# Issuing more feed-forward matmuls as 32-column tiles in a fused attention and feed-forward kernel: from pair 8 on instead of 14

## The chip, the cores and the metric

The kernel runs on one core of one Trainium2 chip. The metric is device microseconds (us) of one execution. Each execution also has a span: the time from its first to its last instruction. It is mostly about 1.8 us shorter than the execution's time. In this document "PE" is TensorE, "DVE" VectorE, "ACT" ScalarE, "POOL" GpSimd and "SP" SyncE. A verdict calls two kernels the same when they are within 2%, so nearly all that follows happens inside "same". It is told because the pieces are not small: a gain and a loss of about 1 us each meet in one place.

## The reference, cut to what matters

```python
q, k, v: (8, 12, 448, 64) float32            # batch, heads, sequence, head dim
scores = q @ k.T / 8;  attn = softmax(scores);  x = attn @ v
x = x.transpose(0, 2, 1, 3).reshape(3584, 768)
g = x @ w_gate;  val = x @ w_val             # (768, 1536) each
out = (g * sigmoid(g) * val) @ w_out         # (1536, 768)
```

There are 96 heads, worked through as 48 pairs. The 3584 rows of x go through the feed-forward part in eight blocks of 384 or 512 rows.

## The kernel before

TensorE's order is written by hand. For each pair `pr` it runs half of the scores (`s`), then in even pairs the row sums of an earlier pair and in odd pairs value products of an earlier pair (`acc`), then some feed-forward steps, then the other half of the scores, and so on. The scores use 64 rows of the array and 128 columns. The sums and value products are issued as four column tiles of 128 rows by 32 columns:

```python
def pv(p0, t, pool=None):
    ...
    for c in range(NC):
        for j in range(4):
            nc.tensor.matmul(acc[ts(j, 32), 0:S], lhsT=v16[g][...], rhs=E[...][:, c, j % 2, :],
                             start=(c == 0), stop=(c == NC - 1))
```

A feed-forward matmul is either one 128x128 matmul or the same work cut into four 128x32 tiles:

```python
def mm(dst, lhsT, rhs, start, stop):
    if not tiled[0]:
        nc.tensor.matmul(dst, lhsT=lhsT, rhs=rhs, start=start, stop=stop)      # line 261
        return
    for j in range(4):
        nc.tensor.matmul(dst[ts(j, 32), :], lhsT=lhsT[:, ts(j, 32)], rhs=rhs,  # line 264
                         start=start, stop=stop)
```

The switch is set in the loop over pairs:

```python
work = odd and pr > FIRST + 1                 # value products in both halves of the pair
...
tiled[0] = pr >= TILED                        # first run, behind sums or value products
carry = ffn_run(...)
...
tiled[0] = pr >= TILED and work               # second run, only in odd pairs
carry = ffn_run(...)
```

The softmax here doesn't subtract the row's maximum and nothing guards it: scores larger than these inputs give would overflow.

## Time and profile before

| what | value | where from |
|---|---|---|
| time, three runs | 463.16 us (462.67 to 463.72) | timed runs |
| span of the profiled execution | 460.2 us | page |
| PE busy | 452.3 us, 98% | page, part 1 |
| next engine | ACT, 53% | page, part 1 |
| chain that ended last | PE 95% | page, part 4 |
| DMA share in the stage changed (pairs 8 to 13) | 1.38 | windows |

PE holds the chain. A busy PE does not mean that PE can't get faster: its records overlap and their ends are modelled. What counts is the distance between the starts of two blocks in the timeline. The DMA share of 1.38 says that in this stage all 16 DMA engines are busy, with more than one packet at a time in the records.

### The profile page before, as it was taken

What the parts mean: (1) busy time and instruction counts of PE and PEld (TensorE: products, weight loads), DVE (VectorE), ACT (ScalarE), POOL (GpSimd) and SP (SyncE); (2) the same over time, 40 slices, a digit from 0 to 9 for tenths busy, and PEclk for the clock granted to TensorE, in tenths of its full rate; (3) what the DMA queues carried; (4) which work ended last, traced back from release to release, by engine and by line L of the source; (5) the groups of instructions that cost most, each with busy time, mean ns of one, the idle gap of its engine ahead of it and who ended that gap; (6) DMA issues with size and microseconds to landing.
All of it is one profiled execution on the core that took longest, in us unless ns stands there. A gap on an engine that the chain in (4) does not pass through costs nothing.

```text
span 460.2 us, 14133 instructions
## 1 busy us (share of the span) xinstructions
PE 452.3 (98%) x6367; PEld 227.8 (49%) x6367; DVE 236.8 (51%) x371; ACT 243.0 (53%) x353; POOL 104.2 (23%) x164
## 2 busy tenths in 40 slices
PE   8899999999999999999999999999999999999996
PEld 3344444444455555444455555544445556554454
DVE  2765663666764554564654554636555546334310
ACT  7986666656664555454646555455555562222222
POOL 8455606334150132303123040210200000000000
PEclk9999999999999999999999999999999999999999
DMA  9999999995793484662758393903603111100123
GB/s 133 195 200 201 192 180 183 223 154 80 90 113 57 78 126 49 114 102 31 118 58 119 67 131 74 142 6 76 98 10 56 37 37 36 36 11 25 36 68 103
DMA packets 82045, 44.23 MB, mean 96 GB/s; under 512 B 36673, under 2 KB 78529, under 8 KB 81985
## 3 DMA queue, kind: packets, MB, share of 16 engines
q0 software_dynamic: 42368, 23.37, 39.2%
q1 hardware_dynamic: 39520, 19.92, 23.8%
q8 instruction: 49, 0.80, 0.7%
q14 instruction: 12, 0.09, 0.1%
q10 hardware_dynamic: 96, 0.05, 0.0%
HBM read 47.19 MB, written 11.01 MB: 126 GB/s over the span
## 4 chain that ended last, share of the span: by engine, by line
PE 95%; ACT 3%; DMA 1%; DVE 0%; issue 0%; SPq 0%; ACTq 0%
PE gp L264 15%; PE op L261 14%; PE vp L264 13%; PE vp L261 11%; PE op L264 10%; PE s L196 10%; PE gp L261 9%; PE acc L212 9%; PE acc L234 4%; ACT E L203 2%; DMA rk<-in_k_dram 1%; PE tp L184 1%; PE wp L103 0%; PE tp L167 0%; DVE qkT L175 0%
## 5 line engine op out<-in xcount | busy, mean ns | idle before, releaser
L203 ACT ACTIVATE E<-s 112x896 f16<-112x896 f32 x192 | 164.6, 917 | 24.3 <-PE s L196 24.1
L280 ACT ACTIVATE sg<-gp 128x384 f32<-128x384 f32 (+1 forms) x96 | 52.3, 545 | 85.4 <-PE gp L264 54.7
L292 DVE SCALAR_TENSOR_TENSOR t<-sg,gp 128x384 f32<-128x384 f32 (+1 forms) x96 | 58.5, 610 | 64.3 <-ACT sg L280 64.2
L325 ACT ACTIVATE osb<-op 128x384 f32<-128x384 f32 (+1 forms) x57 | 27.7, 486 | 100.5 <-PE op L261 56.3
L264 PE MATMUL gp<-X,wg 128*32 128x512 f16 (+1 forms) x1416 | 78.1, 355 | 0.0
L249 DVE RECIPROCAL R<-ssb 128x112 f32<-128x112 f32 x92 | 73.1, 827 | 0.7
L295 DVE SCALAR_TENSOR_TENSOR hts<-t,vp 128x384 f16<-128x384 f32 (+1 forms) x96 | 59.6, 621 | 23.3 <-PE vp L264 7.9
L261 PE MATMUL op<-wo,hts 128*128 128x384 f16 (+1 forms) x408 | 68.6, 322 | 0.0
L264 PE MATMUL vp<-X,wv 128*32 128x512 f16 (+1 forms) x1224 | 66.9, 353 | 0.0
L226 DVE TENSOR_TENSOR X<-acc,R 128x448 f16<-128x448 f32 x48 | 29.7, 624 | 64.9 <-PE acc L212 63.1
L261 PE MATMUL vp<-X,wv 128*128 128x384 f16 (+1 forms) x270 | 58.4, 352 | 0.0
L196 PE MATMUL s<-qkT 64*128 64x448 f16 x384 | 54.8, 355 | 2.5 <-ACT E L203 2.2
L261 PEld LDWEIGHTS <-hts 128*128 128x128 f16 x408 | 38.9, 98 | 28.2 <-issue 3.0
L264 PEld LDWEIGHTS <-wg 128*32 128x32 f16 x1416 | 37.8, 97 | 29.6
L264 PE MATMUL op<-wo,hts 128*32 128x384 f16 x1104 | 48.9, 326 | 0.0
L261 PE MATMUL gp<-X,wg 128*128 128x384 f16 (+1 forms) x222 | 47.4, 350 | 0.0
L264 PEld LDWEIGHTS <-wv 128*32 128x32 f16 x1224 | 32.7, 97 | 25.5
L212 PE MATMUL acc<-E,vt 112*32 112x448 f16 x768 | 45.2, 355 | 0.0
L126 POOL DMA_DIRECT2D vt<-in_v_dram x16 | 12.3, 772 | 142.7 <-PE acc L212 141.7
L261 PEld LDWEIGHTS <-wv 128*128 128x128 f16 x270 | 25.3, 98 | 26.9 <-issue 4.8
L264 PEld LDWEIGHTS <-hts 128*32 128x32 f16 x1104 | 29.5, 97 | 16.3
L154 POOL COPY qk<-q 112x512 f16<-112x512 f16 x37 | 22.9, 620 | 63.9 <-DMA qkT<-qk 46.4
(38 smaller groups left out, 201.2 us busy)
## 6 DMA issues: line engine op xcount, KB each, us to landing
vt<-in_v_dram POOLq DMA_DIRECT2D x16, 336.0 KB, 5.2
q<-in_q_dram POOLq DMA_DIRECT2D x22, 224.0 KB, 5.9
k<-in_k_dram POOLq DMA_DIRECT2D x22, 224.0 KB, 6.7
out_dram<-osb SPq DMA_DIRECT2D x7, 336.0 KB, 3.1
wg<-in_moe_w_gate_dram POOLq DMA_DIRECT2D x8, 288.0 KB, 11.1
wv<-in_moe_w_val_dram POOLq DMA_DIRECT2D x8, 288.0 KB, 11.4
wo<-in_moe_w_out_dram POOLq DMA_DIRECT2D x2, 1152.0 KB, 21.6
out_dram<-osb SPq DMA_DIRECT2D x8, 288.0 KB, 2.9
```

Of the source, the lines that this page charges most:

```text
L154: nc.gpsimd.tensor_copy(dst, src)
L196: nc.tensor.matmul(s[:, hx, 0:S], lhsT=t[ts(hx, 64)].rearrange("p c q -> p (c q)")[:, c * P : c * P + 128], rhs=t[ts(hx, 64), NC:, :].rear ...
L203: nc.scalar.activation(E[pr][:, c], s[0:P, :, 0:S], AF.Exp, scale=sm_scale)
L212: nc.tensor.matmul(acc[ts(j, 32), 0:S], lhsT=v16[g][:, 2 * r + j % 2, c, :].rearrange("p (d t) -> p t d", t=2)[:, t], rhs=E[p0 + j // 2][: ...
L226: nc.vector.tensor_tensor(X[kk][:, hp + t, ts(bb, S)], acc[:, 0:S], R[p0][:], ALU.mult)
L249: lambda i=i: nc.vector.reciprocal(rt[:, ts(i, P)], ssb[:, ts(i, P)]) for i in range(4)
L261: nc.tensor.matmul(dst, lhsT=lhsT, rhs=rhs, start=start, stop=stop)
L264: nc.tensor.matmul(dst[ts(j, 32), :], lhsT=lhsT[:, ts(j, 32)], rhs=rhs, start=start, stop=stop)
L280: nc.scalar.activation(sg[:, 0:n], gp[:, 0:n], AF.Tanh, scale=0.5)
L292: nc.vector.scalar_tensor_tensor(t1[:, 0:n], sg[:, 0:n], 1.0, gp[:, 0:n], ALU.add, ALU.mult)
L295: nc.vector.scalar_tensor_tensor(hts[:, fb, 0:n], t1[:, 0:n], 0.5 * HS, vp[:, 0:n], ALU.mult, ALU.mult)
L325: nc.scalar.activation(osb[:, ds(m0, w)], op[:, 0:w], AF.Copy, scale=1.0 / HS)
```

## The change

A block that follows the 32-column sums or value products in the same tiling should not have to drain the array first. A step from one cutting of the array to another (128x128, 128x32, 64x128) between two matmuls that follow each other is called a mode change below. So the switch to tiles is made six pairs earlier:

```diff
-TILED = 14
+TILED = 8
```

## The prediction

> **What bounds the kernel now.** I read the page first: part 1 (busy time of each engine) and part 4 (the chain that ended last).
>
> ```profile
> PE 452.3 (98%) x6367; PEld 227.8 (49%) x6367; DVE 236.8 (51%) x371; ACT 243.0 (53%) x353; POOL 104.2 (23%) x164
> ...
> PE 95%; ACT 3%; DMA 1%; DVE 0%; issue 0%; SPq 0%; ACTq 0%
> ```
>
> TensorE (PE) is busy for 98% of the 460.2 us span and makes 95% of the chain; the next engine is at 53%. The page warns that ends of matmuls are modelled, so "busy" alone does not say that nothing can be gained inside it. So I took next the waits of PE over the whole run, then the windows view over the stage that the change touches (pairs 8 to 13, which run from 42.27 us, the row sums of pair 8, to 82.58 us, the first scores of pair 14):
>
> ```profile
> PE s L196 <- ACT E L203: 2.2, 5, 0.4
> PE acc L234 <- ACT E L203: 0.4, 1, 0.4
> ...
> 42.27:82.58 40.31, 40.31 (x362) 19.00 (x360) 22.65 (x37) 25.41 (x36) 17.95 (x27) 1.00 1.38 184
> ```
>
> The first two lines are waits in total, their number, and the longest. All of them are before 27 us in the timeline; the waits view restricted to 36 to 90 us lists none. The last line gives busy PE, weight load, DVE, ACT and POOL in us, then the granted clock, DMA share and GB/s. PE is busy in all 40.31 us, at full clock; VectorE has 17.7 us and ScalarE 14.9 us to spare. So what one TensorE block costs is the distance between the starts of two blocks, and that is what I took from the timeline of PE. First the present form in the stage touched:
>
> ```profile
> 56.53 0.94 PE L234 MATMUL acc<-E,ones 112*32 112x448 f16 x16
> 57.41 1.15 PE L261 MATMUL vp<-X,wv 128*128 128x384 f16 x6
> 58.39 1.14 PE L261 MATMUL gp<-X,wg 128*128 128x384 f16 x6
> 59.46 0.55 PE L196 MATMUL s<-qkT 64*128 64x448 f16 x4
> ...
> 62.49 0.94 PE L212 MATMUL acc<-E,vt 112*32 112x448 f16 x16
> 63.36 1.15 PE L261 MATMUL vp<-X,wv 128*128 128x384 f16 x6
> 64.35 2.11 PE L261 MATMUL op<-wo,hts 128*128 128x384 f16 x12
> 66.39 0.55 PE L196 MATMUL s<-qkT 64*128 64x448 f16 x4
> ```
>
> Then the same two patterns later, where the kernel already issues the feed-forward blocks as 32-column tiles (L264, four times as many matmuls):
>
> ```profile
> 158.53 0.94 PE L212 MATMUL acc<-E,vt 112*32 112x448 f16 x16
> 159.30 2.13 PE L264 MATMUL op<-wo,hts 128*32 128x384 f16 x48
> 161.25 1.15 PE L264 MATMUL vp<-X,wv 128*32 128x384 f16 x24
> 162.33 0.55 PE L196 MATMUL s<-qkT 64*128 64x448 f16 x4
> ...
> 360.71 0.94 PE L212 MATMUL acc<-E,vt 112*32 112x448 f16 x16
> 361.48 1.15 PE L264 MATMUL gp<-X,wg 128*32 128x384 f16 x24
> 362.46 1.15 PE L264 MATMUL vp<-X,wv 128*32 128x384 f16 x24
> 363.54 0.55 PE L196 MATMUL s<-qkT 64*128 64x448 f16 x4
> ```
>
> The first column is the start in us. Value products or sums, two 384-wide steps, then scores: 59.46 - 56.53 = 2.93 us untiled and 363.54 - 360.71 = 2.83 us tiled. Value products, one 384-wide step and one output chunk: 66.39 - 62.49 = 3.90 untiled and 162.33 - 158.53 = 3.80 tiled. Tiling takes 0.10 us off a segment, whichever it is. The reader should see where: the 16 matmuls of the acc block are followed after 0.87 to 0.88 us by an untiled block and after 0.77 us by a tiled one. The steps are equally long in both forms (57.41 to 58.39 and 361.48 to 362.46, both 0.98), and so is the exit to the scores (58.39 to 59.46: 1.07; 362.46 to 363.54: 1.08).
>
> **What the Trainium skill says.** (1) "TensorEngine Tiling (Array Packing)", Key Properties: changing the tiling mode, not merely the tile, drains the TensorE. The trace agrees: 0.10 us more where 128x32 is followed by 128x128, and none where 128x32 follows itself. (2) Same page, Restrictions: column tiling disables Fast Weight Load. If that showed, tiled steps would be longer; the trace has one weight load at 97 ns tiled and 98 ns untiled (rows of PEld), and no longer step, so it is hidden here. (3) "TensorE: Matmul & The Clock Gate", Back-to-back issue gap: N / 2.4 + 2.5 ns warm, which is 162.5 ns for 384 columns; the trace has 0.98 us / 6 = 163 ns untiled and the same step as 24 tiled matmuls, 40.8 ns each. (4) Same page, Part 1: a start-to-start floor of about 25 ns, and some 62 ns of ucode per matmul when hardware decode is off. At 40.8 ns the trace is above the first and below the second, so neither floor binds at this width.
>
> **The change, part by part.** The diff lowers one constant, so the first feed-forward run of each pair 8 to 13, and the second one of the odd pairs, is issued tiled; these are the runs that directly follow a sums or value-product block. The second run of the even pairs follows scores and stays untiled.
>
> - *Added instructions.* The instruction order of the built kernels shows 13420 rows on PE in place of 12736. That is 684 more, 342 matmuls and 342 weight loads: 114 untiled matmuls become 456. Their cost is 0, by the equal step lengths above.
> - *Moved.* Nothing. ACT's order is the same; the differences on DVE, POOL and SP are only buffer numbers.
> - *Removed.* The nine blocks in the timeline of before that hold these 114 matmuls start at 43.14, 50.58, 54.00, 57.41, 63.36, 67.75, 71.16, 77.11 and 80.53 us: eight of 12 matmuls and one of 18. Each follows an acc block, and each loses one drain. Counting mode changes along the PE order gives 217 before and 208 after, so nine fewer, none added.
> - *Sum.* The nine distances from acc to untiled add up to 7.86 us (six of 0.87, three of 0.88: 5.22 + 2.64 = 7.86). Eight such distances in the already tiled stretch from 141 to 178 us average 0.767 us; 9 x 0.767 = 6.90. The gain is 7.86 - 6.90 = 0.96 us, 0.107 each.
>
> All of this lies on the path: PE waits for nothing between 27 us and the end, so what it saves early moves all that follows forward. Predicted span 460.2 - 0.96 = 459.2 us; predicted time 463.16 - 0.96 = 462.2 us, that is 0.2%.
>
> **Rivals.**
>
> *A data wait takes the gain back.* This stage has the DMA saturated (share 1.38 above, digits of 9 throughout), so TensorE could run into transfers that do not come sooner. I took each landing (start of the issue plus time to landing) against its first use. Output weights, first half: issued at 44.77, landing 18.1 us later, at 62.9; first used at 64.35. PE will be there five drains sooner, 0.53 us, so 1.5 us of slack becomes 0.95. Second half: 45.8 + 25.0 = 70.8, used at 73.70: 2.9 us. Transposed q and k of pair 11: 48.01 + 9.9 = 57.9, used at 62.01, 4.1 us; pair 14: 73.65 + 4.4 = 78.05, used at 82.58, 4.5 us; pairs 12, 13 and 15 have 6 us or more. All exceed the largest shift, 0.96 us. If the output weights landed 2 us later, about 1 us would be lost and the time would stay at 463.2. I give this 5%.
>
> *Instruction fetch becomes the bound.* Four times as many instructions per us, in the stage with the busiest DMA. Against it: the stage from 82 to 116 us has tiled blocks already and a nearly saturated DMA, and its pitch is that of an unhindered stage:
>
> ```profile
> 94.91 1.47 PE L264 MATMUL gp<-X,wg 128*32 128x512 f16 x24
> 96.21 1.47 PE L264 MATMUL vp<-X,wv 128*32 128x512 f16 x24
> 97.61 0.55 PE L196 MATMUL s<-qkT 64*128 64x448 f16 x4
> ```
>
> The distances 1.30 and 1.40 recur at 340 us with the DMA nearly idle (338.58, 339.88, 341.17, 342.57). The page of that window counts 4 packets of the instruction queue in 34 us; 684 added rows at 256 to a 16 KB packet (64 bytes each, an estimate from 49 packets, 0.80 MB and 14133 instructions) are fewer than 3 packets more. If a fetch did stall PE by about 1 us each, the gain would go and the time would be 463 to 465. I give this 4%.
>
> *Another engine becomes the bound.* The stage gets 0.96 us shorter, 2.4% of 40.31; ACT, the next busiest at 25.41 us, has 14.9 us of idle. PSUM buffers are released in the same order as before, and the tiled stage from pair 14 on, with the same buffers, has no PE wait. It would make the time 462.2 to 463.2; 2%.
>
> *A larger gain.* Were tiled steps themselves shorter by, say, 5%, the 114 matmuls at 163 ns (18.6 us) would yield 0.9 us more, 461.3. The equal steps speak against it.
>
> **Range and chances.** The arithmetic gain is sharp, the times less so: the three runs of before spread from 462.67 to 463.72, so a median of a few runs may be off by 0.4 us on either side, in before and after alike. I put 0.7 us on each side: 461.5 to 462.9. Two per cent is 9.3 us, ten times the gain, and no rival comes near it on either side: faster 0.01, same 0.98, slower 0.01.
>
> **What would show it right or wrong.** Right: acc to L264 distances of 0.76 to 0.77 us at the nine places; tiled 384-wide steps of 0.98 us and chunks of 1.96; 208 mode changes; the scores of pair 14 at 81.6 us in place of 82.58; no PE wait between 30 and 100 us; every later block 0.96 us earlier; a span near 459.2. Wrong: a PE or PEld wait ended by the output weights near 63.8 us, a gap within a tiled block beside an instruction packet, tiled 384-wide steps longer than 0.98 us in this stage, or a shift that is there at 82 us and gone before the end.

## More of the kernel before

Weights are loaded on the way, in an order given by pair. `wo` are the two halves of `w_out`, 1152 KB each as written in float16, and "V" is a group of values (336 KB):

```python
wq = {..., 4: [("g", 3), ("v", 3), ("qk", 12)],
      6: [("V", 3), ("o", 0)],
      7: [("o", 1)]}
```

The first matmul that reads `wo` is an output product of the first block of rows, in the first feed-forward run of pair 11. "The first use of wo" below means this one.

## The result

| | before | changed |
|---|---|---|
| median, six runs each | 463.37 us | 462.40 us |
| range | 462.67 to 463.72 | 462.14 to 463.02 |
| ratio | | 0.9982 (95%: 0.9970 to 0.9995) |
| span of the profiled execution | 460.2 us | 460.4 us |

Ratios throughout are the mean time of one kernel's runs over that of the other's of the same rounds, so not quite the ratio of the medians quoted.

The gain of the medians is 463.37 - 462.40 = 0.97 us; 0.96 was predicted. But the profiled execution of the changed kernel is not shorter than that of before: 460.4 against 460.2 us. Both facts need an explanation, and the agreement of 0.97 with 0.96 turned out to be the less meaningful of the two.

First the page of the changed kernel, parts 1 and 4:

```profile
PE 451.4 (98%) x6709; PEld 229.4 (50%) x6709; DVE 236.8 (51%) x371; ACT 243.0 (53%) x353; POOL 104.2 (23%) x164
...
PE 85%; DMA 12%; POOL 2%; issue 1%; ACT 0%; POOLq 0%
```

There are 342 matmuls more, as foreseen. The chain is new: before it was PE 95% and DMA 1%; now DMA is 12% of it. Something on PE waits for a transfer. The timeline of PE shows the drains first (start in us, duration, engine, line, shapes):

```profile
56.20 0.94 PE L234 MATMUL acc<-E,ones 112*32 112x448 f16 x16
56.97 1.15 PE L264 MATMUL vp<-X,wv 128*32 128x384 f16 x24
57.95 1.15 PE L264 MATMUL gp<-X,wg 128*32 128x384 f16 x24
59.03 0.55 PE L196 MATMUL s<-qkT 64*128 64x448 f16 x4
```

From the sums to the tiled block it is now 0.77 us in place of 0.88, and the whole segment takes 59.03 - 56.20 = 2.83 us in place of 2.93, with steps of 0.98 us as before. The drain is gone as predicted. A few microseconds on, still in the timeline of the changed kernel:

```profile
62.05 0.94 PE L212 MATMUL acc<-E,vt 112*32 112x448 f16 x16
62.82 1.15 PE L264 MATMUL vp<-X,wv 128*32 128x384 f16 x24
64.88 2.13 PE L264 MATMUL op<-wo,hts 128*32 128x384 f16 x48 [0.91 <-DMA wo<-in_moe_w_out_dram]
66.95 0.55 PE L196 MATMUL s<-qkT 64*128 64x448 f16 x4
```

The output product should start 0.98 us after the value step, at 63.80. It starts at 64.88, 1.08 us late, because wo has not landed (0.91 us is the part without any earlier matmul still in the records). The windows view over the same pairs, from the sums of pair 8 to the first scores of pair 14, agrees:

```profile
42.25:82.72 40.47, 39.56 (x704) 20.72 (x704) 22.65 (x37) 25.42 (x36) 17.98 (x27) 1.00 1.41 177
```

The stage takes 40.47 us against 40.31: nine drains fewer, minus 0.96, and one wait more, plus 1.08, make plus 0.12, and 40.31 + 0.12 = 40.43; the rest is rounding and the spread of single distances.

Why does wo land late? The view of wo's transfer, restricted to its first half, gives the start of the issue and the time to landing, first in before, then in the changed kernel:

```profile
L142 POOL DMA_DIRECT2D wo<-in_moe_w_out_dram x1: 1037/1037/1037, 44.8 to 44.8; - x1
DMA to landing us min/median/max: 18.1/18.1/18.1
```

```profile
L142 POOL DMA_DIRECT2D wo<-in_moe_w_out_dram x1: 1037/1037/1037, 44.2 to 44.2; - x1
DMA to landing us min/median/max: 20.6/20.6/20.6
```

It is the same transfer. It was issued 0.5 us sooner and landed 2.0 us later, at 64.8 in place of 62.8 us. The DMA view from 52 to 60 us, in 40 slices of 0.2 us (busy share of the DMA engines in tenths, then GB/s), shows one place where much more time is lost than in before (a shallower dip near 54 us is in both). Before:

```profile
DMA  9999999997999999999999999999999999999999
GB/s 193 189 223 218 179 187 172 173 151 47 173 210 178 184 211 178 184 207 182 182 210 182 180 206 188 195 192 191 188 192 192 189 188 196 186 192 196 188 191 192
```

Changed:

```profile
DMA  9999999999569999999994019999999999999999
GB/s 216 177 192 219 179 170 182 189 132 74 28 87 187 197 187 261 183 177 173 168 36 17 6 14 175 200 184 205 192 192 197 186 191 193 188 192 192 189 188 196
...
q8 instruction: 1, 0.02, 0.7%
```

In the changed kernel there is a hole of four slices near 56 us: 36, 17, 6 and 14 GB/s in place of some 190, with the DMA engines idle (digits 4, 0, 1). About 0.7 us of transfer is lost there. The last line is a packet of the instruction queue, q8, which this window of before does not have. The trace has it at 55.0 us, 1 us ahead of the hole. TensorE now issues more instructions in the same time, and the next packet of them comes sooner. Both kernels have another such hole between 62.7 and 64.4 us, behind the next instruction packet. In before wo has landed by the time most of it comes; in the changed kernel wo is still under way. With slices of 0.55 us over 44 to 66 us, the changed kernel's 136, 27 and 103 GB/s there are some 0.9 us short of 190. So these two holes make about 1.6 of the 2.0 us (an estimate from the slices).

### The profile page after: what moved, and what is told of

It reads as the page before. It is cut to its first block, busy times and chain, and to the rows that moved or that the text cites. A ratio compares the mean times of both kernels' runs of the same rounds, so it can differ in the third digit from the quotient of the medians.

```text
span 460.4 us, 14817 instructions
## 1 busy us (share of the span) xinstructions
PE 451.4 (98%) x6709; PEld 229.4 (50%) x6709; DVE 236.8 (51%) x371; ACT 243.0 (53%) x353; POOL 104.2 (23%) x164
## 4 chain that ended last, share of the span: by engine, by line
PE 85%; DMA 12%; POOL 2%; issue 1%; ACT 0%; POOLq 0%
PE gp L264 15%; PE vp L264 13%; PE op L261 12%; PE op L264 12%; PE vp L261 9%; PE s L196 8%; PE acc L212 7%; PE gp L261 7%; DMA wv<-in_moe_w_val_dram 5%; DMA wo<-in_moe_w_out_dram 4%; PE acc L234 4%; DMA wg<-in_moe_w_gate_dram 2%; POOL q L117 1%; POOL k L117 1%; POOL vt L126 0%
## 5 line engine op out<-in xcount | busy, mean ns | idle before, releaser
L264 PE MATMUL gp<-X,wg 128*32 128x512 f16 (+1 forms) x1512 | 82.7, 353 | 0.0
L264 PE MATMUL vp<-X,wv 128*32 128x384 f16 (+1 forms) x1344 | 72.7, 351 | 0.0
L264 PE MATMUL op<-wo,hts 128*32 128x384 f16 x1344 | 59.5, 326 | 0.9 <-DMA wo<-in_moe_w_out_dram 0.9
L261 PE MATMUL op<-wo,hts 128*128 128x384 f16 (+1 forms) x348 | 57.9, 321 | 0.0
L196 PE MATMUL s<-qkT 64*128 64x448 f16 x384 | 54.8, 355 | 2.5 <-ACT E L203 2.2
L261 PE MATMUL vp<-X,wv 128*128 128x512 f16 (+1 forms) x240 | 52.7, 356 | 0.0
L264 PEld LDWEIGHTS <-wv 128*32 128x32 f16 x1344 | 35.9, 97 | 27.4
L264 PEld LDWEIGHTS <-hts 128*32 128x32 f16 x1344 | 35.8, 97 | 21.1 <-DMA wo<-in_moe_w_out_dram 1.3
L261 PEld LDWEIGHTS <-hts 128*128 128x128 f16 x348 | 33.4, 98 | 23.3 <-issue 1.5
L261 PE MATMUL gp<-X,wg 128*128 128x384 f16 (+1 forms) x198 | 42.8, 352 | 0.0
L246 DVE COPY ssb<-acc 128x448 f32<-128x448 f32 x23 | 14.4, 625 | 40.9 <-PE acc L234 40.9
```

Source lines behind the costliest of these rows:

```text
L196: nc.tensor.matmul(s[:, hx, 0:S], lhsT=t[ts(hx, 64)].rearrange("p c q -> p (c q)")[:, c * P : c * P + 128], rhs=t[ts(hx, 64), NC:, :].rear ...
```

## The experiments

Twelve kernels ran, in three calls of four. Each call had its own runs of before on the same chip, shared by its four kernels. As the effects are a few tenths of a us, I read the spans of all executions as well as the medians: a span does not contain the start of the program.

### Is the gain repeatable, and is wo the cause of the scatter?

`b_again` and `a_again` are the two kernels unchanged. `b_early` and `a_early` load the first half of wo one place sooner:

```diff
-            6: [("V", 3), ("o", 0)],
+            6: [("o", 0), ("V", 3)],
```

Expected of `b_again`:

> The kernel before, unchanged, as a null and for a second profile with the span of each run. Theory A (drains only; nothing waits for the output weights in the usual run of before): spans near 460.2 us as in the first profile, no PE wait after 27 us. Theory B (the first half of the output weights, wo, is a gate: it lands near 64.8 us in most runs and the first profile was a lucky one): spans of 461.2 to 461.9 us, and unless the profile is lucky again a PE wait on wo of about 1 us near 64 us. Time ratio 1.000.

Of `a_again`:

> The changed kernel, unchanged, again. Theory A: nine drains of 0.107 us saved in full, 0.96 us below the null. Theory B: TensorE waits for wo in both kernels, so the five drains saved ahead of the first output matmul are absorbed by the wait and only the four behind it count: 4 x 0.107 = 0.43 us below the null; a PE wait on wo about 0.5 us longer than that of the null.

Of `b_early`:

> The kernel before with the load of wo's first half issued ahead of one load of values (336 KB) instead of behind it. Theory B: wo lands some 2 us or more earlier, no PE wait on it, span near 460.2 us, 1.0 to 1.6 us below the null. Theory A: the same time as the null within 0.3 us.

Of `a_early`:

> The changed kernel with the same earlier load. Both theories: no wait on wo and all nine drains saved, so 0.96 us below b_early (span near 459.2 us). Theory B also: 1.2 to 1.8 us below a_again. Theory A: the same as a_again within 0.3 us.

| kernel | median us | ratio to before (95%) | spans of the six runs |
|---|---|---|---|
| before, 11 runs | 463.05 | | 460.4 to 461.8 |
| b_again | 462.32 | 0.9988 (0.9975 to 1.0000) | 460.2 to 460.6 |
| a_again | 462.56 | 0.9993 (0.9980 to 1.0005) | 460.6 to 461.0 |
| b_early | 463.87 | 1.0017 (1.0003 to 1.0031) | 460.8 to 462.5 |
| a_early | 465.98 | 1.0057 (1.0036 to 1.0078) | 461.8 to 465.3 |

The null, an unchanged copy, taught most. It differs from before by at least as much as `a_again` does, although its text is that of before. The changed kernel's spans lie close together, those of before spread by 1.4 us. The profile of `a_again` has the wait on wo again (1.0 us, at 65.14 us); that of `b_again` has none.

Both early kernels are slower, where theory B expected a gain. The waits view says why (us in total, times, longest), `b_early` first:

```profile
PE acc L212 <- DMA vt<-in_v_dram: 1.5, 1, 1.5
```

```profile
PE acc L212 <- DMA vt<-in_v_dram: 3.0, 1, 3.0
```

The values that were pushed back are needed at 62.67 us, by the value products of pair 8, whose accumulator holds pair 9 as well. In `b_early` they landed at 44.4 + 20.1 = 64.5. I had moved one transfer past another that was nearly as urgent. And the 3.0 us wait in `a_early` cost more than itself. In the windows view (the number behind the engines is the granted clock) the two microseconds after it ran at half clock:

```profile
66.00:68.00 2.00, 2.00 (x28) 1.10 (x24) 0.87 (x2) 0.00 (x0) 0.00 (x0) 0.50 1.28 192
```

So these two say nothing on what a kernel without the wait would do; the next group does.

### The wait taken away, and the drain measured alone

In these four the first block's output product reads gate weights that landed long ago in place of wo. Shapes, instructions and transfers stay the same. The 384 rows of that block come out wrong.

```diff
-    rhs=wo[oh][:, fb, ds(m0 - oh * OH, w)],
+    rhs=(wgv["g", oh][:, fb % NCB] if first else wo[oh][:, fb])[:, ds(m0 - oh * OH, w)],
```

`b_nogate` is before with this edit and `a_nogate` the changed kernel. `untiled_nogate` has, besides,

```diff
-TILED = 8
+TILED = 99
```

and `all_nogate` tiles the second run of the even pairs too, which stands between two score blocks and so keeps its two mode changes:

```diff
-            tiled[0] = pr >= TILED and work
+            tiled[0] = pr >= TILED
```

Expected of `b_nogate`:

> The kernel before, with the output product of the first block of rows reading gate weights that landed long ago in place of wo (same shapes, same instructions, same transfers; 384 of the 3584 rows come out wrong on purpose). Theory B (the landing of wo is what makes the time of before scatter by 1.5 us and what swallows part of the gain): no wait on wo, and all spans within about 0.3 us of 460.3. Theory A (the scatter has another source): spans scatter from 460.3 to 461.8 as before.

Of `a_nogate`:

> The changed kernel with the same replacement (wrong on purpose in the same rows). Theory B: the whole gain of nine drains appears, 0.96 us below b_nogate: spans near 459.3 us, with the scores of pair 14 about 0.96 us earlier than in b_nogate. If a drain is worth less than 0.107 us or tiled steps are longer in this stage, the difference is smaller though nothing waits.

Of `untiled_nogate`:

> a_nogate with no feed-forward step tiled at all (constant 99 in place of 8): 271 mode changes on TensorE in place of 208. If a drain of 0.107 us for each mode change is the whole cost: 63 x 0.107 = 6.7 us more than a_nogate (span near 466.0). If the gain came from something else about the tiles it need not scale with the count.

Of `all_nogate`:

> a_nogate with the second run of the even pairs tiled as well: 1134 matmuls and as many weight loads more, but only two mode changes fewer (206). If only mode changes count: 0.2 us below a_nogate at most. If tiling itself made a step shorter, or the instructions cost something (fetch, issue), it would be off by more: 1134 extra matmuls at even 5 ns each would be 5.7 us.

| kernel | mode changes on PE | median us | ratio to before (95%) | spans, sorted |
|---|---|---|---|---|
| before, 11 runs | 217 | 462.34 | | 460.3 to 461.7 |
| b_nogate | 217 | 463.37 | 1.0010 (0.9996 to 1.0025) | 460.3, 460.6, 461.5, 461.6, 461.7, 461.9 |
| a_nogate | 208 | 461.89 | 0.9987 (0.9974 to 1.0001) | 459.4, 459.5, 459.6, 460.6, 460.8, 460.9 |
| untiled_nogate (4 runs) | 271 | 468.11 | 1.0125 (1.0111 to 1.0138) | 466.1, 466.1, 466.5, 467.2 |
| all_nogate | 206 | 462.52 | 1.0002 (0.9984 to 1.0020) | 459.5, 459.9, 460.7, 460.8, 461.9, 462.2 |

Three things follow.

The scatter is not made by wo. `b_nogate` has no wait on it and still has two groups, near 460.4 and 461.7. Its profile fell on a slow execution (span 461.9), and by 14 us it is 1.63 us behind the first profile, which is nearly all of the 1.7 us between their spans. The same three instruction groups in the timeline, before (quick) and then `b_nogate` (slow):

```profile
5.08 0.39 PE L103 MATMUL wp<-warm 128*128 128x512 f16 x1
5.64 0.75 PE L196 MATMUL s<-qkT 64*128 64x448 f16 x4 [0.16 <-DVE qkT L175]
6.32 0.39 PE L103 MATMUL wp<-warm 128*128 128x512 f16 x1
```

```profile
5.53 0.61 PE L103 MATMUL wp<-warm 128*128 128x512 f16 x1
6.08 0.95 PE L196 MATMUL s<-qkT 64*128 64x448 f16 x4
6.96 0.61 PE L103 MATMUL wp<-warm 128*128 128x512 f16 x1
```

A warm-up matmul takes 0.39 us in one and 0.61 in the other, until about 10 us. The page "TensorE: Matmul & The Clock Gate" of the Trainium skill, Part 1, says that the window which releases the clock runs freely, so that the warm-up ends at another point in each run. These traces agree with it: their records of the granted clock begin, at full clock, at 4.4 us in before and at 10.5 us in `b_nogate`, and there the durations change. (The windows view gives 1.00 before that too, but nothing is recorded there.) In the 14 profiles the record begins at 4.1 to 5.7 us in ten and at 9.4 to 10.5 us in four, those of `b_nogate`, `all_nogate`, `a_split` and `halved`. I call the two kinds quick and slow starts. A quick start is worth some 1.2 us in the means below and 1.6 in these two profiles. Nothing in the change touches it.

Compared within a kind, the whole gain appears once nothing waits: 460.45 - 459.50 = 0.95 us in quick starts (means of two and three spans) and 461.68 - 460.77 = 0.91 in slow ones (four and three). Predicted: 0.96. Against all executions of before, the median of `a_nogate` is only 0.45 us lower, because the two drew different shares of quick starts.

And the drain has its size. Sixty-three mode changes more cost 466.1 - 459.5 = 6.6 us in quick starts, and 63 x 0.107 = 6.7. What the 0.107 us consist of was not separated. In the trace of before, the first weight load behind the sums starts with its block, at 57.40 us, and takes 95 ns; in the changed kernel the first loads start 0.19 us ahead of theirs. So a weight load that cannot go ahead may be a large part of it. In `all_nogate`, 1134 more matmuls at nearly the same count of changes leave the quickest span where it was (459.5 against 459.4), but its median is 0.6 us above that of `a_nogate`, so the added instructions are not free in every execution. The profiled execution of `all_nogate` is a slow one, 462.2, with two gaps on PE of 0.7 and 0.5 us inside the stage; one of them, within a block at 71.09 us, has no releaser but "issue". They may be waits for instructions; that was not settled.

### Where the loss comes from, and a version without it

`post_only` tiles in addition only the four blocks behind the first use of wo, `pre_only` only the five ahead of it:

```diff
 # post_only                                    # first run, then second run of a pair
-            tiled[0] = pr >= TILED
+            tiled[0] = pr >= 12
-            tiled[0] = pr >= TILED and work
+            tiled[0] = pr >= 11 and work
 # pre_only
-            tiled[0] = pr >= TILED
+            tiled[0] = 8 <= pr <= 11 or pr >= 14
-            tiled[0] = pr >= TILED and work
+            tiled[0] = (8 <= pr <= 10 or pr >= 14) and work
```

`a_split` is the changed kernel with the first half of wo in two tiles, loaded one after the other:

```diff
+    wo0b = consts.tile([128, 4, OH], FP16, name="wo0b")   # wo[0] keeps 8 of 12 row groups
...
+            if i == 0:
+                nc.gpsimd.dma_start(dst[:], src[:, 0:8])
+                src, dst = src[:, 8:12], wo0b
...
-    rhs=wo[oh][:, fb, ...]
+    rhs=(wo0b[:, fb - 8] if oh == 0 and fb >= 8 else wo[oh][:, fb])[...]
```

`halved` is before with twice the instructions and no tiles in the first block's gate and value steps:

```diff
-            for cb in range(NCB):
+            for x0, cb in [(x0, cb) for x0 in range(0, n, n // parts) for cb in range(NCB)]:
                 mm(
-                    gp[:, 0:n],
+                    gp[:, ds(x0, n // parts)],          # parts = 2; the same for vp
```

Expected of `post_only`:

> Only the four blocks behind the first use of wo are tiled as well (second run of pair 11, pairs 12 and 13); 213 mode changes. Theory C (by now: a drain is worth 0.107 us wherever it goes; the instructions that tiling adds ahead of the first use of wo bring one more instruction packet into the flight of wo and delay its landing by about 2 us; the scatter of about 1.4 us between executions is made in the first 10 us): no added packet, so wo lands 18 to 19.5 us after its issue as in before, no PE wait on it, and four drains are saved in full: 0.43 us below the kernel before in executions with the same start, spans near 460.0 us with a quick start and 461.3 with a slow one. That is better than the whole change with a quick start (460.6). Theory D (tiles are worth more or less than their drains, instructions do not matter): between before and the changed kernel.

Of `pre_only`:

> Only the five blocks ahead of the first use of wo are tiled as well (pairs 8 to 10 and the first run of pair 11); 212 mode changes. Theory C: wo lands about 20.7 us after its issue, near 65 us, PE waits about 1 us for it with a quick start, and the five drains are lost: spans 460.9 to 461.2 us, 0.5 to 0.8 us ABOVE the kernel before with a quick start, in spite of five drains fewer. Theory D: 0.53 us below before.

Of `a_split`:

> The changed kernel with the first half of wo in two pieces, two thirds and one third, loaded one after the other; the last third is needed 1.3 us later than the first. Theory C: the two thirds land some 2 us before the whole (near 63) and the wait is gone or below 0.3 us: spans 459.4 to 459.8 us with a quick start, 460.8 with a slow one, about 0.9 us below the kernel before. Theory D: no change against the changed kernel (460.6).

Of `halved`:

> The kernel before with the 144 matmuls of the first block's gate and value steps issued as two halves of 192 columns each: 144 matmuls and weight loads more ahead of the first use of wo, no tiles, the same 217 mode changes. Theory C: a third instruction packet between 44 and 66 us, about 0.15 to 0.2 MB less data moved in that window, and wo lands 20 to 21 us after its issue in place of 18.1 to 19.3. Rival E (the delay of wo comes from the tiles themselves, which read their moving operand four times, and not from instructions): wo lands 18 to 19.5 us after its issue as in before. TensorE itself may be up to 1 us slower here, as there are more and shorter matmuls.

| kernel | median us | ratio to before (95%) | spans, sorted | wo: issue + flight = landing | PE wait on wo |
|---|---|---|---|---|---|
| before, 11 runs | 463.33 | | 460.3, 460.3, 460.5, 460.6, then seven from 461.5 to 461.8 | | |
| post_only | 462.03 | 0.9979 (0.9963 to 0.9995) | 459.7, 459.8, 459.9, 460.5, 460.6, 460.8 | 44.9 + 18.2 = 63.1 | none |
| pre_only | 462.82 | 0.9996 (0.9981 to 1.0010) | 460.9 to 461.2, all six | 44.9 + 20.1 = 65.0 | 0.9 us |
| a_split | 461.36 | 0.9967 (0.9948 to 0.9985) | 459.1, 459.4, 459.5, 459.7, 460.8, 460.9 | first piece 43.8 + 17.1 = 60.9 | none |
| halved | 463.19 | 1.0009 (0.9992 to 1.0025) | 461.2 to 462.4 | 44.9 + 19.6 = 64.5 | none |

`post_only` and `pre_only` tell the two theories apart. Four drains fewer behind the first use of wo bring spans of 459.7 to 459.9 in quick starts, where before has 460.3 to 460.6. Its other three, 460.5 to 460.8, are 0.5 us or more below the 461.3 that I expected of slow starts; no profile fell on one of them, so this miss stays open. Five drains fewer ahead of it bring 460.9 to 461.2: more drains saved, and worse than before in quick starts. The timeline of `pre_only` at the place:

```profile
65.08 2.13 PE L264 MATMUL op<-wo,hts 128*32 128x384 f16 x48 [0.86 <-DVE hts L295]
```

The view names DVE here, which is the other thing this matmul needs. But the vp step before it starts at 63.06, so it would start at 64.04 without a wait; it starts at 65.08, just behind the landing of wo at 65.0. This is a wait for several semaphores put down to the wrong one.

`halved` has no added tiles, and still a hole. Its DMA view from 52 to 60 us:

```profile
DMA  9999999999999972089999129999999999999999
GB/s 195 192 211 189 191 187 220 253 177 168 161 83 182 123 23 12 10 131 166 178 204 108 17 15 147 184 189 200 184 189 200 183 195 193 202 184 184 207 182 184
```

Idle slices at 54.8 to 55.4 us follow an instruction packet at 53.5; those at 56.4 to 56.8 us follow a packet of 8 KB of another instruction queue, q14, at 54.6. Two of my expectations for it failed: there were two instruction packets from 44 to 66 us, not three, and wo flew 19.6 us, not 20 to 21. So it shows that such a hole comes without added tiles. By itself it does not show that instructions make the whole delay: 19.6 us is longer than any flight in an untiled kernel (18.1 to 19.3), but shorter than those of the tiled ones (20.1 to 20.9). The rival, that the tiles themselves slow the transfers, is not needed for the hole.

Put together, the times of the wo flight in all profiles where it was loaded whole and in its place are: untiled up to its landing (before, b_again, b_nogate, untiled_nogate, post_only) 18.1, 19.3, 18.6, 18.4, 18.2 us; tiled ahead of it (changed, a_again, a_nogate, all_nogate, pre_only) 20.6, 20.7, 20.9, 20.8, 20.1. The two groups do not overlap. In each of the first five the trace has two packets of the instruction queue from 44 to 66 us, in each of the second five three. The early kernels, where wo is not in its place, look different: it flew 18.5 us in `b_early` and 18.4 in `a_early`, which has one packet more in the flight. But `a_early` issued it 1.1 us later, and it landed 1.0 us later (61.4 against 60.4).

The DMA packets of the traces tell more. For each flight, the time that the DMA fell short of 190 GB/s can be added up (in slices of 0.1 us). It is 0.3 to 1.0 us in the first five, 1.4 in `halved` and 1.7 to 2.7 in the second five. The flight less this time is 17.8 to 18.3, 18.3 and 18.1 to 19.0 us. So of the 2.1 us between the means of the two groups, 1.6 are time in which the DMA stood idle or nearly so; for the other 0.5 the rival stays open.

Not every instruction packet leaves a hole. The DMA view of the changed kernel from 68 to 74 us has a packet, at 69.7 us, and none:

```profile
GB/s 186 196 186 207 203 205 205 205 201 205 201 300 183 188 176 196 184 179 200 191 191 191 198 198 188 212 188 191 198 191 198 191 212 191 188 208 191 195 198 201
...
q8 instruction: 1, 0.02, 1.0%
```

In these traces the holes go together with the DMA transposes that make qkT from pair 11 on. In the changed kernel the first three are under way from 47.5 to 69.2 us, and the next starts at 74.3. The 14 profiles have 86 packets of this queue from 10 to 74 us. Sixty-one started with no transpose under way, and the DMA stayed at 181 GB/s or more for 2.4 us from there. Of the other 25, 23 left a hole of 36 GB/s or less; the two that did not started less than 0.4 us before the last transpose landed. No run took the transposes away, so this is what goes together, and not a cause that was shown.

`a_split` is the version that beats both. It takes the whole change and removes the wait, as the last third of wo is not needed until 1.3 us after the first. Quick spans are 459.1 to 459.7, slow ones 460.8 and 460.9, against 460.3 to 460.6 and 461.5 to 461.8 of before in the same rounds: 0.8 to 1.0 us, as predicted for the change itself. (Its profile fell on a slow start, so that nothing waits with a quick one is read from the spans alone.)

## Why the prediction was right or wrong

The time, 462.4, was inside the range, and the drain is as predicted. One step failed all the same, and the exact agreement of the gain was luck.

**The drain.** Right in each point: 0.77 us in place of 0.87 to 0.88 from acc to a tiled block, steps of 0.98 us in both forms, 208 mode changes. The removal of the wait (0.95 and 0.91 us) and the count of 63 (6.6 us against 6.7) confirm 0.107 us each.

**"Moved. Nothing", and "All of this lies on the path."** This is the step that failed. The order of the instructions did not move, but the transfers did: wo landed 2.0 us later in the profile, and the DMA idled behind instruction packets that came into its flight. I had counted those packets ("fewer than 3 packets more") and asked only whether PE would wait for one. It did not; the data that shared the DMA with it were late. The prediction named "a PE or PEld wait ended by the output weights near 63.8 us" as a sign of being wrong, and it came.

**The first rival, given 5%.** It is what happened in each profile of the changed kernel. I had worked out 1.5 us of slack for wo and 0.95 after the change, from one execution of before, and held the landing fixed. In other executions of untiled kernels wo landed between 62.7 and 64.4 us; in the second profile of before it landed within 0.2 us of its use. The slack was not a property of the kernel. The sentence "If the output weights landed 2 us later, about 1 us would be lost" describes the profile: 2.0 us later, 1.08 us lost.

**The second rival, given 4%.** The evidence against it, the undisturbed pitch of the stage from 82 to 116 us, was sound for what it tested: whether PE waits for instructions. In that stage PE waited for no transfer. It was not nearly saturated throughout, though: the DMA view from 82 to 116 us has 151 GB/s, and none at all for six slices of 0.85 us. Nor do 64 bytes to an instruction come out of the numbers given: 0.80 MB over 14133 instructions is 57 bytes, and 684 rows then make 2.4 packets. The page of the changed kernel counts 52 packets in place of 49, so three.

**The third point from the skill.** The page "TensorE: Matmul & The Clock Gate", Back-to-back issue gap, calls the formula that of an isolated matmul and gives about 131 ns for each of a stream of 512-column matmuls with weight loads. The prediction left this out. Its own lines decide for the formula: 1.30 us for six such matmuls is 217 ns.

**The scatter.** I took 462.67 to 463.72 for noise of 0.4 us on each side of a median. It is a mixture of quick and slow starts. Of the 33 executions of before with known spans, 19 are quick (up to 460.8), 12 slow (461.4 to 461.8) and 2 between. In the changed kernel the 12 executions lie from 460.4 to 461.2. A likely reason is that after a slow start TensorE arrives later at a landing that does not depend on it as much, so its wait is shorter; no profile of the changed kernel fell on a slow start, so this is argued and not shown. The slow profile of `all_nogate` fits: wo landed at 65.7 us, and PE, which did not need it there, came to that place at 66.16, 0.7 us of which it had lost in a gap.

**The gain of 0.97.** Over these executions before has a mean time of 462.81 us and the changed kernel of 462.53, a gain of 0.28 us. They were run at other times. A plain copy of before was itself below it. The first six runs of before, 462.67 to 463.72, look mostly like slow starts. So the change is worth about nothing after a quick start (460.4 to 460.6 against 460.6 and more) and something after a slow one, and some 0.3 us on average; the full 0.96 us needs wo out of the way.

## What to carry to other kernels

Next to work in a narrow column tiling, wide matmuls can be cut into tiles of the same width with steps as long as before (0.98 us here), and each mode change saved was worth 0.107 us here; count the changes and multiply. But the cut multiplies instructions by four, and their packets share the DMA with the data; here the DMA idled behind them while DMA transposes were under way. Ahead of a transfer that lands just in time, look at the slack in several executions, or split the transfer so that its last part is needed later. Before a difference of a few tenths of a us is believed, run a plain copy, and compare executions of the same kind.

## What the Trainium skill lacked or had wrong

- "TensorEngine Tiling (Array Packing)", Key Properties, says that changing the mode drains TensorE, and names no cost. Measured: 0.107 us from one change in the timeline, and 6.6 us for 63 of them.
- The same page, Performance Considerations, does not say that a wide 128-column matmul may be cut into four column tiles at no loss: 0.98 us for six matmuls of 384 columns and for the 24 tiles, with weight loads of 98 and 97 ns.
- "Runtime: NRT & Kernel Launch", Instruction fetch mechanics, calls the cost of crossing to the next block of instructions mostly hidden; neither it nor another page describes an effect on data transfers. In the traces, 23 of 25 packets of 16 KB that started while a DMA transpose was under way were followed, about 1 us later, by 0.7 to 1.2 us of lost transfer, and none of the 61 others. A 1152 KB transfer under way took 20.1 to 20.9 us with three packets around it and 18.1 to 19.3 with two. What links packet, transpose and idle engines stays open.
- "TensorE: Matmul & The Clock Gate", Part 1, says that the ramp penalty is below 1% of a typical span and not worth fitting. Here the difference between two starts is some 1.2 us of 460, or 0.3%, which was more than the effect under study. The same Part puts the return to half clock behind an idle window of about 3.4 us; here a shorter wait, of 3.0 us, was followed by two microseconds at a granted clock of 0.50.
